# A DeltaNet and maxout kernel on one core: the output product of the last two token groups in seven half-size products instead of eight

## The chip, the cores and the metric

The kernel runs on one core of a Trainium2 chip. The metric is the time of one execution on the device in microseconds (us), the median of several executions. A profiled execution of the same program gives the durations that are used below; all of them are of one run.

## The reference

Four batches, eight heads, 768 positions and a head dimension of 48. A DeltaNet recurrence makes `y`; its heads side by side are 3072 tokens of 384 values; a maxout layer of width 768 with three weights and an output weight follows. Everything is float32.

```python
for t in range(S):
    y[:, :, t] = einsum('bhd,bhde->bhe', q[:, :, t], state)
    v_old = einsum('bhde,bhd->bhe', state, k_n[:, :, t])
    state = state + beta_t * einsum('bhd,bhe->bhde', k_n[:, :, t], v[:, :, t] - v_old)
x = y.transpose(0, 2, 1, 3).reshape(B * S, H * D)          # 3072 x 384
h = maximum(maximum(x @ w1, x @ w2), x @ w3)               # 3072 x 768
out = h @ w_out                                            # 3072 x 384
```

## The kernel before

The sequence is cut into 12 chunks of 64 positions. Two chunks of all four batches make a group of 512 tokens; there are six groups, `m` = 0 to 5. The recurrence of a group and the maxout layer of the group before it are written out in turns: `ffn(m)` (L903) is a generator that yields after each piece of the layer, and the loop at L1173 puts, after yield number `i`, the pieces of the recurrence of group `m + 1` that the table `LINKS` (L1064) names for `i`. The whole order is by hand; each engine executes its own instructions in the order in which they were written, and waits on semaphores where another engine has to be done.

In group 4, whose turns hold the recurrence of group 5, these entries matter. `s0 y0` at 8: the state update (L789) and `y` of chunk 10. `k1 q1` at 10: the products of keys and queries with the state (L731). `u1 w0` at 11: the product `p_u` (L759), and the four reads by which `y` of chunk 10 comes back from DRAM in another order (`read_y`, L850, on SP's queue). `y1 x1` at 13: the product `p_y` (L801), the addition that makes `y` of chunk 11 (L803, VectorE), and its two writes to DRAM (`y_blocks`, L839, SP's queue). `X0 w1` at 14: the transpose of chunk 10 into `xt` (`turn_y`, L861, VectorE), and the four reads of chunk 11. `X1` at 17: the transpose of chunk 11 into `xt`. Group 5 cannot start before it: its layer reads `xt` of 512 tokens at once. Group 5 itself has no recurrence beside it.

The layer of a group has two parts. In the first, each of six tiles of the hidden width has, from group 1 on, two products `p_h` of 128x128 weights with 512 tokens (L914, three matmuls each): w1 was subtracted from w2 and w3 early in the kernel, so the maximum is a relu of the first difference (L924, ScalarE) and a maximum of that with the second (L928, VectorE), and what w1 adds is put back in the output. So twelve of the yields, 0 to 11, are those of the twelve products.

The second part (L938 to L956) makes the output for the four tiles of 128 tokens: a sum of nine matmuls `p_o` with 384 columns each, six of the hidden tiles `h` with `wo_sb` (the output weight), and three of `xt` with `w_sb[0]`, whose columns 0 to 383 hold w1 times w_out since group 1 (`both_layers`, L891). Its columns 384 to 767 are not read after that. ScalarE copies each sum out (L952), and two DMAs on SP's queue store it (L955). Each of the four has a yield inside and one at its end: yields 12 to 19.

`p_h` and `p_o` take turns in two PSUM banks (`ps_ffn`, L80): a tile takes the bank of the tile two before it, once that has been read. Tiles of the pools `work` are handed on in the same way; `tmp` (L543) has two buffers in the solver of the recurrence, where one instruction writes it (L552) and the next reads it (L556). A float32 matmul of the source is two MATMUL instructions in the trace, each with its own weight load (LDWEIGHTS); a transpose is one.

Of the kernel before, what the change touches and what calls it, by code (L numbers as in the profile page):

```python
# [9 lines left out]
FP32 = mybir.dt.float32  # L10
# [4 lines left out]
ALU = mybir.AluOpType  # L15

C = 64
# [6 lines left out]
def kernel(  # L24
# [31 lines left out]
    nc = tc.nc  # L56

    B, H, S, D = q.shape
    NCH = S // C
    DM = H * D  # L60
    DFF = moe_w1.shape[1]
    KT = DM // 128
    FT = DFF // 128
    NP = H // 2
    UNITS = NCH * 2
    GROUPS = UNITS // 4
# [5 lines left out]
    work = ctx.enter_context(tc.tile_pool(name="work", bufs=2))  # L72
# [7 lines left out]
    def ps_ffn(shape, name):  # L80
        return psum.tile(shape, FP32, name=name, tag="ffn", bufs=2)
# [27 lines left out]
    def rows(bb):  # L109
        return slice(C * bb, C * (bb + 1))  # L110
# [70 lines left out]
    for bb in range(2):  # L181
        nc.gpsimd.affine_select(
            out=mask[rows(bb)], in_=mask[rows(bb)], pattern=[[1, C]], base=-1,
# [4 lines left out]
    t1 = [const.tile([128, 2, H, BL], FP32, name=f"t1{i}") for i in range(NU)]  # L188
# [5 lines left out]
    w_sb = [const.tile([128, KT, DFF], FP32, name=f"w{i}_sb") for i in range(3)]  # L194
    wo_sb = const.tile([128, FT, DM], FP32, name="wo_sb")
    pieces = []
    for f in range(FT):
        for w_t, w in zip(w_sb, (moe_w1, moe_w2, moe_w3)):
            bits = w.bitcast(U32).rearrange("(p t) f -> p t f", p=128)
            cols = slice(f * 128, (f + 1) * 128)  # L200
# [106 lines left out]
    def square(name):  # L307
        return work.tile([128, H, C], FP32, name=name, tag="square", bufs=17)
# [39 lines left out]
    def load_blocks(n, queue=nc.gpsimd):  # L348
        c, g = divmod(n, 2)
        for i in range(2):  # L350
            if n % 4 == 2:
                t = kmore[i].rearrange("p a h d -> p (a h d)")[:, 0 : 2 * TURNED]
                t = t.rearrange("p (b x) -> p b x", b=2)
            else:
                t = work.tile(
                    [128, 2, TURNED], FP32, name="turned", tag="w_bits", bufs=5
                )
            turned[n, i] = t
            nc.gpsimd.memset(t[:, :, TURNED - 48 : TURNED], 0.0)  # L359
            for bb in range(2):  # L360
                for par in range(2):
                    for db in range(2):
                        p0, at = DP * par + 32 * db, 32 * (1 - db)
                        (queue, nc.gpsimd)[i].dma_start(  # L364
                            out=t[p0 : p0 + 32, bb, at : at + NP * 2 * D].rearrange(
                                "p (j x) -> p j x", j=NP
                            ),
                            in_=(k, q)[i][
                                2 * bb + g, :, c * C : (c + 1) * C, :
                            ].rearrange(  # L370
                                "(j two) (r tb) d -> two r j (tb d)", two=2, tb=2
                            )[par],
                        )
# [69 lines left out]
    def in_rows(t):  # L443
        return t.rearrange("p s r -> p (s r)")[:, 0 : BL * BL].rearrange(
            "p (j i) -> p j i", i=BL
        )
# [51 lines left out]
    def solve(m):  # L498


        x = in_rows(xs[m])
# [38 lines left out]
        for j in range(size - 1):  # L540
            a, b = j + 1, size - 1 - j
            n = BL // size
            tmp = work.tile([128, 256], FP32, name="tmp")  # L543
            t_v = tmp[:, 0 : n * a * b].rearrange("p (s c i) -> p s c i", s=n, i=b)
            row, column, rest = (
                xv[:, :, j, None, j + 1 : size],
                yv[:, :, 0:a, j, None],
                yv[:, :, 0:a, j + 1 : size],
            )
            if n == 1:  # L550
                row, column, rest, t_v = (t[:, 0] for t in (row, column, rest, t_v))
            nc.vector.tensor_tensor(  # L552
                out=t_v, in0=row.to_broadcast(t_v.shape),
                in1=column.to_broadcast(t_v.shape), op=ALU.mult,
            )
            nc.vector.tensor_tensor(out=rest, in0=rest, in1=t_v, op=ALU.subtract)  # L556
            if m == 1 and j == BL - 8:
                nc.scalar.copy(done[:, :, 0:HB], y[:, :, 0:HB])
            elif m == 1 and j == BL - 2:
                nc.vector.tensor_copy(done[:, :, HB:BL], y[:, :, HB:BL])  # L560
            yield
        if m == 0:
# [3 lines left out]
            for i in range(4):  # L566
                if i % 2:
                    n = H * (i == 3)
# [7 lines left out]
        for cc in range(2):  # L576
            nc.sync.dma_start(
                out=y_d[cc].rearrange("f b h i j -> (f b h) i j"),
                in_=done[64 * cc : 64 * (cc + 1)],
            )  # L580
        yield
        for cc in range(2):
            for half in range(2):
                for bb in range(2):
                    r0 = C * bb + BL * half
                    (one_queue if m or cc else both_queues)[bb].dma_start(
                        out=ut[cc][
                            r0 : r0 + BL, :, :, BL * half : BL * (half + 1)
                        ].rearrange("p g h i -> p (g h) i"),
                        in_=y_d[cc, half, 2 * bb : 2 * bb + 2].rearrange(  # L590
                            "b h c i -> c (b h) i"
                        ),
# [126 lines left out]
    xts, rhss, qss, us, yts = {}, {}, {}, {}, {}  # L719
# [171 lines left out]
    def both_layers(t):  # L891
        p_m = ps_ffn([128, DM], "p_m")
        for f in range(FT):
            nc.tensor.matmul(  # L894
                p_m,
                w_sb[0][:, t, f * 128 : (f + 1) * 128],
                wo_sb[:, f],
                start=(f == 0),
                stop=(f == FT - 1),
            )  # L900
        nc.scalar.copy(w_sb[0][:, t, 0:DM], p_m)

    def ffn(m):  # L903
        xt = xts[m]
        hs = {}

        def hidden(f, lo, w):
            if f not in hs:
                hs[f] = square("h").rearrange("p h c -> p (h c)")
            h = hs[f][:, lo : lo + w]  # L910
            for i in range(m > 0, 3):
                p_h = ps_ffn([128, TOK], "p_h")[:, 0:w]
                for t in range(KT):
                    nc.tensor.matmul(  # L914
                        p_h,
                        w_sb[i][:, t, f * 128 : (f + 1) * 128],
                        xt[:, t, lo : lo + w],
                        start=(t == 0),
                        stop=(t == KT - 1),
                    )  # L920
                if i == 0:
                    nc.scalar.copy(h, p_h)
                elif m and i == 1:
                    nc.scalar.activation(  # L924
                        out=h, in_=p_h, func=mybir.ActivationFunctionType.Relu
                    )
                else:
                    nc.vector.tensor_tensor(out=h, in0=h, in1=p_h, op=ALU.max)  # L928
                yield


        early = FT // 2 if m == 0 else 0
        for lo in (0, TOK // 2):
            for f in range(early):
                yield from hidden(f, lo, TOK // 2)
        for f in range(early, FT):
            yield from hidden(f, 0, TOK)
        for i in range(4):  # L938
            cc, g = divmod(i, 2)
            p_o = ps_ffn([128, DM], "p_o")  # L940
            last = slice(i * 128, (i + 1) * 128)
            terms = [(hs[f][:, last], wo_sb[:, f]) for f in range(FT)]
            if m:
                terms += [(xt[:, t, last], w_sb[0][:, t, 0:DM]) for t in range(KT)]
            for n, (stays, moves) in enumerate(terms):
                nc.tensor.matmul(  # L946
                    p_o, stays, moves, start=(n == 0), stop=(n == len(terms) - 1)
                )
                if m and n == 4:
                    yield  # L950
            o_sb = work.tile([128, DM], FP32, name="o_sb")
            nc.scalar.copy(o_sb, p_o)  # L952
            for bb in range(2):
                tok0 = (2 * bb + g) * S + (2 * m + cc) * C
                nc.sync.dma_start(out=out[tok0 : tok0 + C, :], in_=o_sb[rows(bb)])  # L955
            yield  # L956
# [3 lines left out]
    def some(gen, n):  # L960
        for _ in range(n):
            if next(gen, gen) is gen:
                break
# [74 lines left out]
    for _ in range(2):  # L1038
# [50 lines left out]
        t=turn, K=load_k, L=lambda n: load_blocks(n, nc.sync),  # L1089
        g=lambda n: gram(n, queues=(nc.gpsimd,) * 2 if n in (10, 11) else one_queue),  # L1090
# [82 lines left out]
    for m in range(1, GROUPS):  # L1173
        for i, _ in enumerate(ffn(m)):
            if i == 0:
                some(solving, 3)
            if m == 1 and i in (2, 5, 8):
                both_layers(i // 3)
            if m + 2 < GROUPS:
                if i == 6:  # L1180
                    blocks(m + 2)
                if i == 8:
                    solving = solve(m + 2)
            links(m + 1, LINKS.get(i, ""))
            if i > 7:
                some(solving, 3 if i > 8 else 1)
# [29 lines left out]
```

## Time and profile before

| | us |
|---|---|
| median of 5 runs | 517.62 (515.58 to 521.85) |
| the profiled execution | 514.79 |
| its span, first to last instruction | 512.8 |
| TensorE (PE) busy in the span | 492.1 |
| VectorE (DVE) busy | 305.8 |
| ScalarE (ACT) busy | 163.3 |
| GpSimd (POOL) busy | 192.2 |

In the table of instruction groups, each row has the source line, engine and operation, the tiles (written <- read), the shape, the count, then busy time, mean ns of one, and the idle time of the engine before them:

```profile
L914 PE MATMUL p_h<-xt,w_sb 128*128 128x512 f32 (+1 forms) x522 | 217.7, 561 | 2.5 <-issue 1.8
L946 PE MATMUL p_o<-wo_sb,h 128*128 128x384 f32 x288 | 97.8, 489 | 0.0
L946 PE MATMUL p_o<-w_sb,xt 128*128 128x384 f32 x120 | 42.0, 486 | 0.0
L952 ACT COPY o_sb<-p_o 128x384 f32<-128x384 f32 x24 | 11.5, 478 | 132.1 <-PE p_o L946 126.0
out_dram<-o_sb SPq DMA_DIRECT2D x48, 96.0 KB, 2.2
```

The mean of one matmul is its latency with a modelled end; consecutive matmuls overlap, so that what one costs in a row of many is the busy time of the row by its count: 97.8 us by 288 is 340 ns. The last line is of the list of DMAs: the stores of the output, 48 of them of 96 KB, 2.2 us from issue to landing.

### The profile page before, as it was taken

To read this page: it belongs to the slowest core of one execution; us is meant where nothing else is said; L and a number is where in the kernel's file an instruction comes from. 1 tells how busy PE (TensorE), PEld (TensorE's weight loads), DVE (VectorE), ACT (ScalarE), POOL (GpSimd) and SP (SyncE) were. 2 spreads that over 40 slices of the span, in tenths; PEclk is the share of its full clock that TensorE was granted. 3 is DMA by queue.
4 is the path that set the end of the run, shared out by engine and by line. 5 is a ranking of instruction groups with operands and counts; after the bars stand their busy time and mean duration, and the time that the engine had idled before them with its cause. 6 is when DMAs were issued, how large, how long until landed. Compare 5 with 4: busy or idle time off the path is not lost.

```text
span 512.8 us, 18005 instructions
## 1 busy us (share of the span) xinstructions
PE 492.1 (96%) x7836; PEld 304.4 (59%) x7836; DVE 305.8 (60%) x689; ACT 163.3 (32%) x302; POOL 192.2 (37%) x317
## 2 busy tenths in 40 slices
PE   7678899999999999999999999999999999999996
PEld 6567678755565555565655665555655555654453
DVE  5888998869995521998644897727895331111100
ACT  5476855792431332100252201332001411011000
POOL 7425483773683908650757850513110000000000
PEclk9758899999999999999999999999999999999999
DMA  8927989772065916443845444834243102210011
GB/s 113 203 48 213 202 174 144 194 233 50 20 160 136 180 22 144 122 118 77 174 102 130 137 114 120 148 56 107 55 122 77 24 6 61 78 46 0 0 31 31
DMA packets 105277, 53.45 MB, mean 104 GB/s; under 512 B 89712, under 2 KB 98960, under 8 KB 105200
## 3 DMA queue, kind: packets, MB, share of 16 engines
q1 hardware_dynamic: 93616, 31.55, 30.6%
q0 software_dynamic: 9472, 20.37, 16.1%
q8 instruction: 61, 1.00, 0.9%
q10 hardware_dynamic: 2112, 0.39, 0.5%
q14 instruction: 16, 0.13, 0.1%
HBM read 39.17 MB, written 13.11 MB: 102 GB/s over the span
## 4 chain that ended last, share of the span: by engine, by line
PE 77%; DVE 11%; ACT 4%; DMA 4%; issue 2%; SPq 1%; POOL 0%; DVEq 0%; ACTq 0%; POOLq 0%
PE p_h L914 34%; PE p_o L946 23%; PE p_g L406 3%; PE p_u L759 3%; PE p_m L894 2%; DVE tmp L552 2%; PE p_y L801 2%; PE p_k L731 2%; DVE y_bl L556 2%; PE p_s L782 2%; PE p_t L329 2%; PE p_j L714 2%; DMA qall<-in_q_dram 2%; PE p_q L731 1%; PE p_z L701 1%
## 5 line engine op out<-in xcount | busy, mean ns | idle before, releaser
L914 PE MATMUL p_h<-xt,w_sb 128*128 128x512 f32 (+1 forms) x522 | 217.7, 561 | 2.5 <-issue 1.8
L914 PEld LDWEIGHTS p_h<-xt,w_sb 128*128 128x128 f32 x522 | 95.2, 191 | 87.2 <-issue 80.5
L946 PE MATMUL p_o<-wo_sb,h 128*128 128x384 f32 x288 | 97.8, 489 | 0.0
L928 DVE TENSOR_TENSOR h<-h,p_h 128x512 f32<-128x512 f32 (+1 forms) x48 | 29.6, 617 | 89.8 <-PE p_h L914 89.2
L946 PEld LDWEIGHTS p_o<-wo_sb,h 128*128 128x128 f32 x288 | 53.7, 190 | 35.7 <-issue 0.5
L552 DVE TENSOR_TENSOR tmp<-x_bl,y_bl 128x31 f32<-128x31 f32 (+20 forms) x139 | 51.3, 369 | 4.1
L952 ACT COPY o_sb<-p_o 128x384 f32<-128x384 f32 x24 | 11.5, 478 | 132.1 <-PE p_o L946 126.0
L556 DVE TENSOR_TENSOR y_bl<-y_bl,tmp 128x31 f32<-128x31 f32 (+20 forms) x139 | 48.5, 349 | 4.8
L924 ACT ACTIVATE h<-p_h 128x512 f32<-128x512 f32 x30 | 17.9, 597 | 88.3 <-PE p_h L914 86.7
L946 PE MATMUL p_o<-w_sb,xt 128*128 128x384 f32 x120 | 42.0, 486 | 0.0
L364 POOL DMA_DIRECT2D turned<-in_q_dram x72 | 39.1, 551 | 4.4 <-POOL turned L359 2.9
L254 POOL TENSOR_TENSOR w_sb<-mant,up 128x384 int32<-128x384 int32 x18 | 18.8, 1046 | 38.0 <-DVE mant L250 35.5
L946 PEld LDWEIGHTS p_o<-w_sb,xt 128*128 128x128 f32 x120 | 22.8, 190 | 15.9
L406 PEld LDWEIGHTS p_g<-kqt 48*64 48x64 f32 x1216 | 24.8, 143 | 9.2 <-issue 6.0
L406 PE MATMUL p_g<-kqt 48*64 48x64 f32 (+1 forms) x1216 | 27.9, 243 | 0.9 <-ACT kqt L335 0.8
L120 POOL DMA_DIRECT2D kpad<-in_k_dram x32 | 21.8, 690 | 13.9 <-issue 12.7
L789 DVE TENSOR_TENSOR st<-st,p_s 48x768 f32<-48x768 f32 (+1 forms) x18 | 17.1, 949 | 15.0 <-PE p_s L782 14.8
L139 POOL DMA_DIRECT2D v_t<-in_v_dram x14 | 11.5, 829 | 35.7 <-PE p_u L759 35.7
L390 DVE TENSOR_TENSOR pt<-p_g,mask 128x512 f32<-128x512 f32 x20 | 13.8, 689 | 16.3 <-PE p_g L406 16.3
L287 POOL TENSOR_TENSOR v_t<-v_t,nrm 128x768 f32<-128x768 f32 x12 | 17.9, 1492 | 9.0 <-DVE nrm L281 8.9
L359 POOL MEMSET turned<- 128x96 f32 x18 | 3.3, 191 | 47.7 <-DVE kqt L380 47.7
L759 PEld LDWEIGHTS p_u<-v_t,ut 64*64 64x64 f32 x768 | 13.5, 141 | 9.7 <-issue 8.3
(143 smaller groups left out, 615.6 us busy)
## 6 DMA issues: line engine op xcount, KB each, us to landing
out_dram<-o_sb SPq DMA_DIRECT2D x48, 96.0 KB, 2.2
w_bits<-in_moe_w_dram SPq DMA_DIRECT2D x9, 384.0 KB, 4.8
w_bits<-in_moe_w_dram POOLq DMA_DIRECT2D x9, 384.0 KB, 5.8
turned<-in_q_dram POOLq DMA_DIRECT2D x72, 48.0 KB, 2.8
kpad<-in_k_dram POOLq DMA_DIRECT2D x32, 96.0 KB, 6.5
y_x<-y SPq DMA_DIRECT2D x16, 192.0 KB
qall<-y_x SPq DMA_DIRECT2D x32, 96.0 KB, 2.6
v_t<-in_v_dram POOLq DMA_DIRECT2D x14, 192.0 KB, 5.1
```

What stands on the lines that cost most here:

```text
L120: queues[bb].dma_start(out=dst[rows(bb ^ g), :, 0:D], in_=src[2 * bb + g, :, c * C : (c + 1) * C, :].rearrange("h p d -> p h d"),)
L254: nc.gpsimd.tensor_tensor(out=dst.bitcast(I32), in0=mant_v.bitcast(I32), in1=up_v, op=ALU.add)
L287: nc.gpsimd.tensor_tensor(out=vts[c], in0=vts[c], in1=nrm[:, :, :, None].to_broadcast([128, 2, H, D]), op=ALU.mult,)
L364: (queue, nc.gpsimd)[i].dma_start(out=t[p0 : p0 + 32, bb, at : at + NP * 2 * D].rearrange("p (j x) -> p j x", j=NP), in_=(k, q)[i][2 * bb ...
L406: nc.tensor.matmul(p_g[rows(bb ^ (g * i)), par, c0 : c0 + C * (1 + whole)], kq[:, 0], kq if whole else kq[:, i],)
L552: nc.vector.tensor_tensor(out=t_v, in0=row.to_broadcast(t_v.shape), in1=column.to_broadcast(t_v.shape), op=ALU.mult,)
L556: nc.vector.tensor_tensor(out=rest, in0=rest, in1=t_v, op=ALU.subtract)
L759: nc.tensor.matmul(p_v[rows(bb ^ g), g, i], ut[c % NU][rows(bb), g, h], rhs[rows(bb), g, h],)
L914: nc.tensor.matmul(p_h, w_sb[i][:, t, f * 128 : (f + 1) * 128], xt[:, t, lo : lo + w], start=(t == 0), stop=(t == KT - 1),)
L924: nc.scalar.activation(out=h, in_=p_h, func=mybir.ActivationFunctionType.Relu)
L928: nc.vector.tensor_tensor(out=h, in0=h, in1=p_h, op=ALU.max)
L946: nc.tensor.matmul(p_o, stays, moves, start=(n == 0), stop=(n == len(terms) - 1))
```

## The change

The four output sums of the last two groups are replaced; groups 0 to 3 stay as they are. In `outputs(m, hs)`, the `h` of 512 tokens and 768 hidden values is taken as two by two blocks (256 tokens by 384), and the weight as two by two blocks (384 by 192). Seven products of blocks, with sums and differences of blocks before and after them, take the place of the eight of the ordinary way (Winograd's form of Strassen's method). The part of `xt` (four products of 256 tokens by 384 by 192) is added inside PSUM to four of the sums. Each product is six matmuls with 192 columns, for two tiles of 128 tokens and three tiles of the inner width, into one half each of a PSUM bank; 11 such products of six matmuls make 66, where there were 36 of 384 columns.

The two banks are held through the whole part as `p` and `q`. ScalarE copies four of the results out, VectorE makes the sums, and eight DMAs store the four blocks. `outputs` yields after each of the 11 products, so that its yields are numbers 12 to 22. `cross_weights` makes the four differences of the weight blocks on VectorE, in two parts after yields 8 and 9 of group 4: one of them in place in `wo_sb`, two in the free columns of `w_sb[0]`, one in the tiles `mant`, whose earlier use is over. `tmp` has one buffer instead of two in the whole kernel, which makes room for a new tile `m1`.

```diff
-            tmp = work.tile([128, 256], FP32, name="tmp")
+            tmp = work.tile([128, 256], FP32, name="tmp", bufs=1)
...
+    def cross_weights(part):
+        left, right = slice(0, HALF), slice(HALF, DM)
+        top, bottom = wo_sb[:, 0:PAIRS], wo_sb[:, PAIRS:FT]
+        spare = w_sb[0][:, :, DM : 2 * DM]
+        minus = nc.vector.tensor_tensor
+        if part == 0:
+            minus(out=spare[:, :, right], in0=bottom[:, :, right], in1=top[:, :, right], op=ALU.subtract)
+            minus(out=top[:, :, right], in0=top[:, :, right], in1=top[:, :, left], op=ALU.subtract)
+            return
+        minus(out=spare[:, :, left], in0=bottom[:, :, right], in1=top[:, :, right], op=ALU.subtract)
...
+        for j in range(PAIRS):
+            minus(out=fourth[j], in0=wo_sb[:, PAIRS + j, left], in1=spare[:, j, left], op=ALU.subtract)
...
+    def outputs(m, hs):
...
+        p, q = (ps_ffn([128, 2, HALF], "p_o") for _ in range(2))
+        def times(to, a, b, start=True, stop=True):
+            for g in range(2):
+                for j in range(PAIRS):
+                    nc.tensor.matmul(to[:, g], a[j][:, 128 * g : 128 * (g + 1)], b[j], ...)
...
+        times(p, a11, w["b11"])                        # yield 12
+        m1 = held("m1", 1); nc.scalar.copy(m1, p)
+        yield
...
+        for j in range(PAIRS): op(s32[j], a11[j], a21[j], minus)
+        for j in range(PAIRS): op(s14[j], a21[j], a22[j], plus)
+        times(q, a12, w["b21"], True, False)           # yield 13
+        yield
+        x_times(q, 0, 0)                               # yield 14
+        c11 = held("o_sb", 2); op(c11, m1, q, plus); store(c11, 0, 0)
+        yield
+        times(p, s32, w["t3"])                         # yield 15
+        m7 = held("o_sb", 2); nc.scalar.copy(m7, p)
+        yield
+        times(q, s14, w["t1"])                         # yield 16
+        m5 = held("up", 2); nc.scalar.copy(m5, q)
+        for j in range(PAIRS): op(s32[j], s14[j], a11[j], minus)
+        yield
+        times(p, s32, w["t2"])                         # yield 17
+        m6 = held("up", 2); nc.scalar.copy(m6, p)
+        for j in range(PAIRS): op(s14[j], a12[j], s32[j], minus)
+        yield
+        x_times(q, 0, 1, True, False)                  # yield 18
+        op(m6, m6, m1, plus); op(m7, m7, m6, plus)
+        yield
+        times(p, a22, w["t4"], True, False)            # yield 19
+        op(m6, m6, m5, plus); op(m5, m5, m7, plus)
+        yield
+        x_times(p, 256, 0)                             # yield 20
+        op(m7, m7, p, plus); store(m7, 1, 0)
+        yield
+        times(q, s14, w["b22"], False)                 # yield 21
+        op(m6, m6, q, plus); store(m6, 0, 1)
+        yield
+        x_times(p, 256, 1, True)                       # yield 22
+        op(m5, m5, p, plus); store(m5, 1, 1)
+        yield
...
+        if m >= GROUPS - 2:
+            yield from outputs(m, hs)
+            return
...
+            if m == GROUPS - 2 and i in (8, 9):
+                cross_weights(i - 8)
```

Statements that the source has on lines of their own are joined here, and the numbers of the yields are added. `op` is an elementwise VectorE instruction, `store` two DMAs on SP's queue, each of 64 partitions with two pieces of 768 bytes (before: one piece of 1536 bytes).

More of the change, by code (lines that the diff above doesn't have):

```diff
@@ L901, in both_layers @@
         nc.scalar.copy(w_sb[0][:, t, 0:DM], p_m)
+    HALF = DM // 2
+    PAIRS = FT // 2
+    crossed = {}
+    def cross_weights(part):
[4 more added lines that the diff above has]
+        if part == 0:
+            minus(
+                out=spare[:, :, right], in0=bottom[:, :, right], in1=top[:, :, right],
+                op=ALU.subtract,
+            )
+            minus(
+                out=top[:, :, right], in0=top[:, :, right], in1=top[:, :, left],
+                op=ALU.subtract,
+            )
+            return
+        minus(
+            out=spare[:, :, left], in0=bottom[:, :, right], in1=top[:, :, right],
+            op=ALU.subtract,
+        )
+        fourth = []
+        for n in range(2):
+            t = work.tile([128, DM], FP32, name="mant", bufs=2)
+            for i in range(2 - n):
+                fourth.append(t[:, HALF * i : HALF * (i + 1)])
+        for j in range(PAIRS):
+            minus(
+                out=fourth[j], in0=wo_sb[:, PAIRS + j, left], in1=spare[:, j, left],
+                op=ALU.subtract,
+            )
+        crossed.update(
+            b11=[top[:, j, left] for j in range(PAIRS)],
+            b21=[bottom[:, j, left] for j in range(PAIRS)],
+            b22=[bottom[:, j, right] for j in range(PAIRS)],
+            t1=[top[:, j, right] for j in range(PAIRS)],
+            t2=[spare[:, j, left] for j in range(PAIRS)],
+            t3=[spare[:, j, right] for j in range(PAIRS)],
+            t4=fourth,
+        )
@@ new lines, in outputs, with x_times, held, store @@
+    def outputs(m, hs):
+        xt, w = xts[m], crossed
+        a11, a21, a12, a22 = (
+            [hs[j + d][:, lo : lo + 256] for j in range(PAIRS)]
+            for d, lo in ((0, 0), (0, 256), (PAIRS, 0), (PAIRS, 256))
+        )
+        p, q = (ps_ffn([128, 2, HALF], "p_o") for _ in range(2))
+        def times(to, a, b, start=True, stop=True):
+            for g in range(2):
+                for j in range(PAIRS):
+                    nc.tensor.matmul(
+                        to[:, g], a[j][:, 128 * g : 128 * (g + 1)], b[j],
+                        start=(start and g == j == 0),
+                        stop=(stop and g == 1 and j == PAIRS - 1),
+                    )
+        def x_times(to, lo, right, start=False, stop=True):
+            times(
+                to,
+                [xt[:, t, lo : lo + 256] for t in range(KT)],
+                [w_sb[0][:, t, HALF * right : HALF * (right + 1)] for t in range(KT)],
+                start, stop,
+            )
+        def held(name, dtype_bufs):
+            return work.tile([128, 2, HALF], FP32, name=name, bufs=dtype_bufs)
+        def store(o, cc, right):
+            cols = slice(HALF * right, HALF * (right + 1))
+            s0 = (2 * m + cc) * C
+            for n in range(2):
+                nc.sync.dma_start(
+                    out=out.rearrange("(b s) d -> b s d", s=S)[
+                        2 * n : 2 * n + 2, s0 : s0 + C, cols
+                    ].rearrange("g c x -> c g x"),
+                    in_=o[rows(n)],
+                )
+        def op(to, a, b, how):
+            nc.vector.tensor_tensor(out=to, in0=a, in1=b, op=how)
+        plus, minus = ALU.add, ALU.subtract
+        times(p, a11, w["b11"])
+        m1 = held("m1", 1)
+        nc.scalar.copy(m1, p)
+        yield
+        sums = [square("s").rearrange("p h c -> p (h c)") for _ in range(PAIRS)]
+        s14, s32 = ([s[:, lo : lo + 256] for s in sums] for lo in (0, 256))
+        for j in range(PAIRS):
+            op(s32[j], a11[j], a21[j], minus)
+        for j in range(PAIRS):
+            op(s14[j], a21[j], a22[j], plus)
+        times(q, a12, w["b21"], True, False)
+        yield
+        x_times(q, 0, 0)
+        c11 = held("o_sb", 2)
+        op(c11, m1, q, plus)
+        store(c11, 0, 0)
+        yield
+        times(p, s32, w["t3"])
+        m7 = held("o_sb", 2)
+        nc.scalar.copy(m7, p)
+        yield
+        times(q, s14, w["t1"])
+        m5 = held("up", 2)
+        nc.scalar.copy(m5, q)
+        for j in range(PAIRS):
+            op(s32[j], s14[j], a11[j], minus)
+        yield
+        times(p, s32, w["t2"])
+        m6 = held("up", 2)
+        nc.scalar.copy(m6, p)
+        for j in range(PAIRS):
+            op(s14[j], a12[j], s32[j], minus)
+        yield
+        x_times(q, 0, 1, True, False)
+        op(m6, m6, m1, plus)
+        op(m7, m7, m6, plus)
+        yield
+        times(p, a22, w["t4"], True, False)
+        op(m6, m6, m5, plus)
+        op(m5, m5, m7, plus)
+        yield
+        x_times(p, 256, 0)
+        op(m7, m7, p, plus)
+        store(m7, 1, 0)
+        yield
+        times(q, s14, w["b22"], False)
+        op(m6, m6, q, plus)
+        store(m6, 0, 1)
+        yield
+        x_times(p, 256, 1, True)
+        op(m5, m5, p, plus)
+        store(m5, 1, 1)
+        yield
```

## The prediction

> **What bounds the kernel now.** I read first the busy table and the 40 slices of the page, then the chain of waits in order of time for the last 90 us, then the timeline there by engine.
>
> ```profile
> PE   7678899999999999999999999999999999999996
> DVE  5888998869995521998644897727895331111100
> PEclk9758899999999999999999999999999999999999
> ```
>
> TensorE is busy in nine tenths or more of nearly every slice, at full granted clock; VectorE is nearly empty in the last six slices, where the change lies. The chain of waits (start us, length us, what):
>
> ```profile
> 425.85 2.77 PE p_h L914 x6
> 428.62 1.08 PE p_u L759 x64
> 429.70 6.00 PE p_o L946 x18
> 435.70 1.08 PE p_y L801 x64
> 436.78 17.61 PE p_o L946 x54
> 454.39 30.90 PE p_h L914 x72
> 485.29 23.23 PE p_o L946 x72
> 508.53 0.03 ACTq L952
> 508.56 0.04 issue
> 508.60 0.48 ACT o_sb L952
> ```
>
> It is TensorE without a gap from 425 us to the last copy. So a microsecond taken from a `p_o` there is a microsecond of the time, until some wait appears. The output part of group 4 is 6.00 + 17.61 = 23.61 us, that of group 5 23.23 us, each of 72 instructions.
>
> **The matmuls.** Before, 72 instructions of 384 columns take 23.23 / 72 = 322.6 ns each; the 72 of 512 columns take 30.90 / 72 = 429.2 ns. Six of 256 columns:
>
> ```profile
> 71.77 1.46 PE L914 MATMUL p_h<-xt,w_sb 128*128 128x256 f32 x6
> 43.77 0.92 PE L820 MATMUL p_x<-ident,y 128*128 128x128 f32 x6 [0.78 <-DVE y L805]
> 43.74 0.76 PEld L820 LDWEIGHTS p_x<-ident,y 128*128 128x128 f32 x6 [0.87 <-ACT root_bl L261]
> ```
>
> One of 256 has a latency of 379 ns, so the step is (1.46 - 0.379) / 5 = 216 ns. The slope is (322.6 - 216) / 128 = 0.833 ns a column, and 512 columns lie on that line. At 192 columns it gives 216 - 64 x 0.833 = 162.7 ns. After, a group has 66 matmuls, 132 instructions: 132 x 0.1627 = 21.47 us instead of 23.23. Columns fall by a twelfth (66 x 192 against 36 x 384), and 60 more instructions give a little of that back. **Gain: 1.76 us in each group, 3.52 us in all.**
>
> That stands if the weight loads keep up. The load of a `p_o` matmul lasts 190 ns in the trace, longer than 162.7, and every matmul has its own. The third line above shows that a load's duration is not its pace: six loads of 195 ns each in 0.76 us, a step of (0.76 - 0.195) / 5 = 113 ns, at a granted clock of 1.00, with matmuls of 128 columns between. These are transposes, one instruction each, but their loads are the longer kind. The first matmuls of the kernel (`p_w`, L977), ordinary float32 with 128 columns, run slower in every part, with loads of 333 ns and latencies of 421, and 12 of them take 2.93 us: at most (2.93 - 0.421) / 11 = 228 ns a step, again well under the load. So the price of a step lies between 162.7 and 190 ns (the full duration of a load); I take 162.7, since both rows with narrower matmuls stay well under their load's duration.
>
> **Group 4, in time.** A product of six matmuls is 12 x 0.1627 = 1.95 us. With the 0.19 us that `p_o` loses at each change from the recurrence's products (6.00 - 18 x 0.3226, and the same once more in the 17.61), products 1 and 2 end at 433.80, `p_y` at 434.88, and products 3 to 11 at 437.02, 438.98, 440.93, 442.88, 444.83, 446.78, 448.74, 450.69 and 452.64. Now the waits. VectorE's prices: 384 elements 0.55 us (L871 551 ns in SBUF; between L928's 408 and 686 ns for 256 and 512 out of PSUM), 256 elements 0.42 (L552), 0.03 between two.
>
> The six sums before product 4 begin after the last maximum, at 429.45, and take 6 x 0.45 = 2.7 us: done by 432.2, needed at 437.02. The sums for product 6 wait for product 4 (438.98), come behind the transpose of chunk 10 (1.23 us from 437.7) and end at 440.5; product 6 starts at 440.93 and wants only the first of them. ScalarE's copies of four sums (0.48 us each) have a whole product's time. These cost nothing; without that cover each would cost what it is late, some tenths.
>
> The transpose of chunk 11 is another matter:
>
> ```profile
> 437.89 1.16 SPq L839 DMA_DIRECT2D y_x<-y  x2
> 444.70 2.54 SPq L850 DMA_DIRECT2D qall<-y_x  x4
> 449.07 1.25 DVE L861 STREAM_TRANSPOSE xt<-qall 128x768 f32<-128x768 f32 x1 [10.07 <-DMA qall<-y_x]
> ```
>
> `y` goes to DRAM, the reads wait for that, and VectorE stood 10.07 us before the transpose, with nothing behind it. After the change `p_y` ends 1.90 us earlier (434.88 for 436.78), so the transpose starts at 447.17 and ends at 448.42. The store of the first block is now queued on SP between the writes and the reads; it goes out by 438.9 and the reads wait until 442.8 anyway. But behind the transpose VectorE now has four sums of 384 (2.32 us, to 450.77) and then the sum that reads bank `p` after product 9, done at 451.32. Product 11 writes that bank and should start at 450.69: with 0.05 us for the semaphore it starts at 451.37. **Stall: 0.68 us**, from none (transpose 0.7 us earlier) to some 2.2 (1.5 later, since a store of 192 KB, now in smaller pieces, shares the queue with the writes).
>
> Product 11 ends at 453.32, and the first `p_h` of group 5 takes the same bank `p`: it waits for the last sum, 0.13 us (the time from `p_y`'s end to its reader, 436.91 - 436.78) + 0.55 + 0.05 = **0.73 us**. Before, the bank of the next tile had been read a product earlier. `p_h` starts at 454.05 instead of 454.39: group 4 gains 0.35.
>
> The Trainium skill, "Perfetto Trace Analysis", section Optimizing Tensor Performance, says that independent groups of matmuls should rotate through banks so that a copy overlaps the next group. The place just priced breaks that rotation once; the rows above give its cost, the page gives none.
>
> **Group 5.** No recurrence stands between, so the same order has no late transpose; the sum out of `p` after product 9 starts at once, a product ahead of its need. At the end VectorE's sum (0.13 + 0.55) stands where ScalarE's copy stood (0.07 + 0.48): +0.13. The two last stores are of the same size and the issue took 0.56 us for 128 rows (L839) and 0.59 for 64 (L955), so I take the tail of DMA as unchanged (0 to 0.5 more). Group 5 gains 1.76 - 0.13 = 1.63.
>
> **At nothing.** The weight differences: in part one, two instructions of 576 elements, 0.75 us each (from 551 ns for 384 and 1225 for 1024, L538), in VectorE's wait of 2.71 us before the state update at 417.63; part two, 0.75 + 3 x 0.35 + gaps = 1.9 us, after the maximum that ends at 422.06 and before the subtraction at 425.04, an idle of 2.98. If that cover were gone, up to 1.5 us would fall on `p_u`. The single `tmp`: each multiplication in the solver waits for the subtraction before it already, since it reads the row that it wrote; both stand in one engine's order. SP's other stores have nobody behind them.
>
> **Sum.** -0.35 - 1.63 = -1.98 us: 512.8 for the profiled execution of 514.79 us. The median of the runs is 0.55% above that execution, so the same ratio gives 515.6 against 517.62.
>
> **Rivals.** (1) *The loads set the pace: slower.* At 190 ns a step a group's products take 25.08 us, 1.85 more than before; the stall at product 11 disappears (its bank is read in time), the wait of the first `p_h` and the tail stay: 2 x 1.85 + 0.73 + 0.13 = +4.56, 522.2 us. It decides from about 170 ns a step (1.98 us over 264 instructions above 162.7). For it: the load lasts longer than the matmul, in ordinary matmuls at full clock never seen before. Against: the two rows of narrow matmuls. Chance 0.10.
> The harder form of it, load and matmul one after the other, would be 190 + 162.7 ns a step, 46.6 us a group and some 564 us; chance 0.01, as 72 instructions with loads of 190 ns already go by at 322.6, on the line of the columns alone. The Trainium skill, "TensorE: Matmul & The Clock Gate", section Part 3, has that form as a rule: a load overlaps running matmuls only where their row groups differ. By that rule the present step could not be what it is, all loads being of 128 rows; the trace disagrees.
> (2) *The late transpose costs more.* If `y` returns 1.5 us later than I shift it, product 11 and group 5 start that much later: 514.3 and, scaled, 517.1. For it: the write waits 5.6 us on its landing and now shares the time with a store. Chance 0.22.
> (3) *No stall at product 11*, the transpose 0.7 us or more earlier: 0.68 less, 514.9. Chance 0.13.
> That the change does not do what it says is excluded: the built order has 66 matmuls of 192 columns in each of the two groups.
>
> **How the numbers follow.** My forecast has 0.50; 0.04 is for what I have not seen, on both sides. About 1% is what a measurement of this kernel can tell from no change: the runs before lie between -0.4% and +0.8% of their median. All likely cases lie within 1%. Slower by over 1%: half of rival 1, which stands at +0.9%, its harder form, and a little of rival 2 and the unseen: 0.08. Faster by over 1%: the forecast at -0.4% and rival 3 at -0.5% with the scatter of a median, and the unseen: 0.07. Range: from 3 us below the forecast (no stall, and 2 us of scatter) to 519.6, which takes in rival 2 with its scatter and leaves out most of rival 1.
>
> **What would show it.** The `p_o` of group 5 in the chain of waits at about 21.5 us with 132 instructions, its loads starting about 163 ns apart; VectorE's transpose of chunk 11 near 447 and idle on the DMA; product 11 of group 4 waiting on VectorE for some 0.7 us, and the first `p_h` of group 5 for as much. Wrong if group 5's part is 25 us, if the `p_h` before the output part grow, or if the stores at the end land later than 2.2 us after issue.

## The result, and the profile after

| | us |
|---|---|
| median before / after | 516.81 / 515.92 |
| ratio of the runs after to those before | 0.9981, 95% interval 0.9969 to 0.9992 |
| forecast | 515.6 (512.6 to 519.6) |
| the profiled execution after, and its span | 517.23, 515.3 |

The change makes the kernel about 1.0 us faster (0.19% of 516.81; 0.4 to 1.6 by the interval). The profiled execution after happens to be longer than that of before; it is 3.4 us late already at 433.12 us, where the output part of group 4 begins (429.70 before), and 2.7 us of that are there at 98.5 us (the first instruction of L871, 95.8 before), long before the output parts that were changed. The other profiles read here begin the part between 430.4 and 434.4 us (three_groups aside), the kernel with nothing but the single `tmp` buffer latest, so the stretches are compared from there on. The profile of the run named after_again fell into a disturbed execution (granted clock 0.83) and is not read below; its times are.

The chain of waits in order of time of the changed kernel (start us, length us, what):

```profile
432.04 1.08 PE p_u L759 x64
433.12 2.16 PE p_o L960 x12
435.28 0.02 issue
435.30 0.49 ACT m L994
435.79 2.63 issue
438.42 0.96 DVE y L803
...
439.99 6.43 DMA y_x<-y
...
447.76 1.70 SPq L850
...
449.51 2.58 DMA qall<-y_x
...
452.11 1.22 DVE xt L861
...
455.66 0.57 DVE o_sb L989
...
456.27 2.22 PE p_o L960 x12
458.49 30.90 PE p_h L1057 x72
489.38 21.46 PE p_o L960 x132
510.85 0.02 issue
510.87 0.56 DVE up L989
```

Before, this stretch was TensorE alone. Now the chain leaves TensorE in the first products of group 4 and goes through `y` of chunk 11, its way to DRAM and back, the transpose and VectorE's sums, and returns to TensorE only for product 11. (The 2.63 us called issue are a gap in what the chain could follow: meanwhile TensorE ran product 2 and `p_y`, which ended at 437.14 + 1.15 = 438.29 us, just before VectorE made `y`.) Group 4 took 454.39 - 429.70 = 24.69 us from the end of `p_u` to the first `p_h` of group 5; it takes 458.49 - 433.12 = 25.37: 0.68 us more. Group 5's 132 instructions take 21.46 instead of 23.23 us, 1.77 less. From the last matmul to the end of the span it is 515.3 - 510.85 = 4.45 us, before 512.8 - 508.53 = 4.27: 0.18 more. Together 0.68 - 1.77 + 0.18 = -0.91 us, or 0.9982 of the 514.79 of the profiled execution before, inside the measured interval.

The timeline by engine (start us, length us, engine, line, work, count, in brackets the idle before and what ended it):

```profile
437.14 1.15 PE L801 MATMUL p_y<-u,pt 64*64 64x48 f32 x64
446.48 3.64 SPq L850 DMA_DIRECT2D qall<-y_x  x4
452.11 1.22 DVE L861 STREAM_TRANSPOSE xt<-qall 128x768 f32<-128x768 f32 x1 [7.29 <-DMA qall<-y_x]
453.26 0.52 DVE L989 TENSOR_TENSOR up<-up,m 128x384 f32<-128x384 f32 x1
453.81 0.56 DVE L989 TENSOR_TENSOR o_sb<-o_sb,up 128x384 f32<-128x384 f32 x1
454.40 0.56 DVE L989 TENSOR_TENSOR up<-up 128x384 f32<-128x384 f32 x1
454.99 0.56 DVE L989 TENSOR_TENSOR up<-up,o_sb 128x384 f32<-128x384 f32 x1
455.66 0.56 DVE L989 TENSOR_TENSOR o_sb<-o_sb,p_o 128x384 f32<-128x384 f32 x1
458.52 0.56 DVE L989 TENSOR_TENSOR up<-up,p_o 128x384 f32<-128x384 f32 x1 [1.85 <-PE p_o L960]
456.27 2.22 PE L960 MATMUL p_o<-w_sb,xt 128*128 128x192 f32 x12 [2.18 <-DVE o_sb L989]
458.32 1.88 PE L1057 MATMUL p_h<-xt,w_sb 128*128 128x512 f32 x4
```

VectorE stands 7.29 us before the transpose, and four sums and the one that frees bank `p` come behind it. Product 11 waits 2.18 us for that sum. The last two lines hold a second thing: the first `p_h` of group 5 writes from 458.32 on, before the sum of 458.52 has read bank `p`. So it uses the other bank, `q`, and does not wait for that sum.

### The profile page after: what moved, and what is told of

Read it like the earlier page. It is cut to its first block, busy times and chain, and to the rows that moved or that the text cites. A ratio compares the mean times of both kernels' runs of the same rounds, so it can differ in the third digit from the quotient of the medians.

```text
span 515.3 us, 18314 instructions
## 1 busy us (share of the span) xinstructions
PE 493.7 (96%) x7956; PEld 322.6 (63%) x7956; DVE 325.7 (63%) x735; ACT 163.5 (32%) x302; POOL 192.7 (37%) x317
## 4 chain that ended last, share of the span: by engine, by line
PE 81%; DVE 7%; DMA 5%; ACT 2%; issue 2%; SPq 1%; POOL 0%; DVEq 0%; POOLq 0%; ACTq 0%
PE p_h L1057 37%; PE p_o L1092 17%; PE p_o L960 5%; PE p_g L406 4%; DMA qall<-in_q_dram 3%; PE p_u L759 2%; PE p_m L894 2%; PE p_k L731 2%; PE p_s L782 2%; PE p_j L714 2%; PE p_y L801 2%; PE p_q L731 1%; PE p_t L329 1%; PE p_z L701 1%; DMA y_x<-y 1%
## 5 line engine op out<-in xcount | busy, mean ns | idle before, releaser
L1092 PE MATMUL p_o<-wo_sb,h 128*128 128x384 f32 x192 | 65.3, 490 | 0.0
L1092 PEld LDWEIGHTS p_o<-wo_sb,h 128*128 128x128 f32 x192 | 35.7, 190 | 23.2
L1098 ACT COPY o_sb<-p_o 128x384 f32<-128x384 f32 x16 | 7.7, 478 | 86.1 <-PE p_o L1092 80.0
L1092 PE MATMUL p_o<-w_sb,xt 128*128 128x384 f32 x72 | 25.2, 486 | 0.0
L1092 PEld LDWEIGHTS p_o<-w_sb,xt 128*128 128x128 f32 x72 | 13.7, 190 | 9.5
L960 PE MATMUL p_o<-w_sb,xt 128*128 128x192 f32 x96 | 17.1, 328 | 2.2 <-DVE o_sb L989 2.2
```

Source lines behind the costliest of these rows:

```text
L960: nc.tensor.matmul(to[:, g], a[j][:, 128 * g : 128 * (g + 1)], b[j], start=(start and g == j == 0), stop=(stop and g == 1 and j == PAIRS - 1),
L1092: nc.tensor.matmul(p_o, stays, moves, start=(n == 0), stop=(n == len(terms) - 1))
```

## The experiments

Each is the changed kernel with the edit shown, unless it says otherwise; the edits are shown shortened. A ratio is against the kernel before on the same chip. "Group 4's part" is the time from the end of `p_u` to the first `p_h` of group 5.

**The parts alone.** First the changed kernel again, then the seven products in one of the two groups.

> The changed kernel once more, beside the parts of it. Theory A (the matmuls gain 1.76 us in each group; in group 4 the wait for the late transpose of chunk 11 takes more than that back): group 5's output part again 21.46 us, group 4's between the end of p_u and the first p_h of group 5 about 25.4 us (24.7 before), and some 1.0 us less in the ratio (0.998). Theory B (the stall of 2.2 us before product 11 was an accident of that one profile, in which one read of y took 1.70 us to issue instead of 0.60): group 4's part about 24 us here.

Ratio 0.9938 (0.9910 to 0.9966): below the 0.998 of theory A; theory B gives both groups 0.996 (under g5_only).

```diff
-        if m >= GROUPS - 2:
+        if m == GROUPS - 2:
             yield from outputs(m, hs)
...
+            if m == GROUPS - 1 and i == 8:      # wo_sb as it was
+                nc.vector.tensor_tensor(out=top_right, in0=top_right, in1=top_left, op=ALU.add)
```

> The seven products in group 4 alone; group 5 is made in the old way, after one more instruction on VectorE restores the block of wo_sb that was changed in place. Theory A: group 4's part is 0.7 us longer than before, nothing else moves, so +0.7 us (ratio 1.001). Theory B: group 4's part gains about 0.4 to 1.1 us (ratio 0.998 to 0.999).

Ratio 1.0001 (0.9975 to 1.0027). Chain and timeline of this kernel:

```profile
430.53 1.08 PE p_u L759 x64
456.82 30.90 PE p_h L1057 x72
487.72 23.23 PE p_o L1092 x72
454.61 2.22 PE L960 MATMUL p_o<-w_sb,xt 128*128 128x192 f32 x12 [2.02 <-DVE o_sb L989]
444.95 3.54 SPq L850 DMA_DIRECT2D qall<-y_x  x4
```

Group 4's part is 456.82 - 431.61 = 25.21 us, 0.52 more than before, with a wait of 2.02: the stall is no accident of one profile. The seven products in group 4, in this order, gain nothing.

```diff
-        if m >= GROUPS - 2:
+        if m >= GROUPS - 1:
             yield from outputs(m, hs)
...
-            if m == GROUPS - 2 and i in (8, 9):
+            if m == GROUPS - 1 and i in (8, 9):
                 cross_weights(i - 8)
```

> The seven products in group 5 alone (the weight differences are made on VectorE in group 5). Theory A: the whole gain lies here: 1.76 us less for the matmuls, 0.2 us more at the end, -1.6 us (ratio 0.997), more than both groups together. Theory B: less than both groups together, ratio 0.997 against 0.996 for both.

Ratio 0.9972 (0.9945 to 1.0000), group 5 again 21.46 us, group 4 as before (458.22 - 433.52 = 24.70). So the trace is as theory A has it. The times do not bear it out: by A this kernel gains more than both groups together, and on this chip both together came out lower (0.9938), with intervals that overlap.

**The late transpose out of the way.** One entry of the order is moved: the transpose of chunk 11 (`X1`) from behind yield 17 to behind yield 20, where the sum that frees bank `p` already stands in VectorE's order:

```diff
-            links(m + 1, LINKS.get(i, ""))
+            names = LINKS.get(i, "")
+            if m == GROUPS - 2:
+                names = {17: "", 20: "X1"}.get(i, names)
+            links(m + 1, names)
```

> The changed kernel with one thing moved: in group 4 the transpose of chunk 11 stands on VectorE behind the sum that frees bank p after product 9 (yield 20 instead of 17). Theory A: product 11 no longer waits, 2.2 us less than the changed kernel, group 4's part about 23.2 us, -3.1 us against before (ratio 0.994). Theory B: nothing or up to 0.7 us less than the changed kernel. A third theory (the first p_h of group 5 waits for xt instead, since the transpose now ends later): the stall moves to the first p_h and the time stays at 0.998.

Ratio 0.9945 (0.9920 to 0.9970), as theory A gave it. Its timeline and chain:

```profile
450.24 0.56 DVE L989 TENSOR_TENSOR o_sb<-o_sb,p_o 128x384 f32<-128x384 f32 x1 [2.95 <-PE p_o L960]
450.71 1.22 DVE L861 STREAM_TRANSPOSE xt<-qall 128x768 f32<-128x768 f32 x1
431.17 4.10 PE p_o L960 x24
435.27 1.08 PE p_y L801 x64
436.35 17.75 PE p_o L960 x108
454.10 30.90 PE p_h L1057 x72
485.00 21.46 PE p_o L960 x132
```

TensorE is the chain again without a gap; group 4's part is 454.10 - 431.17 = 22.93 us, 1.76 less than before, just the gain that was worked out for the matmuls, and 25.37 - 22.93 = 2.44 us less than in the changed kernel: the wait of 2.18 us, and 0.27 us that product 11 took longer behind it. The transpose finds its data already there, and `p_h` does not wait for it. Since the changed kernel had come out alike in the same comparison (0.9938), both were measured once more on one chip.

> The changed kernel once more, on one chip with x1_late, as the two came out alike in the first comparison (0.994 both) although the traces show a stall of 2.2 us in one and none in the other. Theory A (the stall is real and costs its length): ratio about 0.998 here. Theory B (it is there in some executions only, or is paid back elsewhere): the same ratio as x1_late. The trace: 1.4 to 2.2 us of wait before product 11 of group 4.

Ratio 0.9978 (0.9952 to 1.0005); the wait before product 11 is 1.99 us.

> Theory A: about 2 us less than the changed kernel on the same chip, ratio 0.994. Theory B: as the changed kernel. The trace: no wait before product 11, group 4's part 22.9 us, group 5's 21.46.

Ratio 0.9928 (0.9894 to 0.9962), no wait, group 4's part 455.65 - 432.73 = 22.92 us. So theory A: in the traces the stall costs its length and a little more. The times bear this out in this comparison (0.9978 and 0.9928, with intervals that still overlap a little) and did not in the first (0.9938 and 0.9945). The 0.9938 of the changed kernel stands beside 0.9981, the most exact, and 0.9978; what made it so low is not known, and a comparison of this size is uncertain by some 0.3% either way.

**What made the transpose late.** The store of the first block is moved behind the reads on SP's queue, with the transpose in its old place:

```diff
         op(c11, m1, q, plus)
-        store(c11, 0, 0)
         yield
+        store(c11, 0, 0)
         times(p, s32, w["t3"])
```

> The changed kernel with the store of the first block queued on SP behind the four reads of chunk 11 instead of before them. The theory (the store shares the way with the write of y and delays its landing, and with it the transpose and product 11): from the write's issue to the first read 6.8 us as before the change (7.05 with the store between), so the transpose starts 0.25 us earlier relative to p_y; if the third read issues in 0.6 us too (1.7 in the profile of the changed kernel), 1.3 us earlier and the stall at product 11 falls to about 0.9 us. The rival (the write's time does not depend on the store): 7.05 us and a stall of 1.0 or 2.1 us, depending on the third read alone.

One execution (514.88 us; the kernel before beside it 516.52, the median of 7):

```profile
438.00 1.14 SPq L839 DMA_DIRECT2D y_x<-y  x2
444.81 2.53 SPq L850 DMA_DIRECT2D qall<-y_x  x4
449.89 1.24 DVE L861 STREAM_TRANSPOSE xt<-qall 128x768 f32<-128x768 f32 x1 [6.46 <-DMA qall<-y_x]
454.05 2.22 PE L960 MATMUL p_o<-w_sb,xt 128*128 128x192 f32 x12 [1.36 <-DVE o_sb L989]
```

From the write's issue to the first read it is 444.81 - 438.00 = 6.81 us, as before the change (444.70 - 437.89), against 446.48 - 439.40 = 7.08 with the store between. The theory holds for that quarter of a microsecond, and the other profiles read here bear it out: this time is 7.00 to 7.10 us in the eight with the store between, 6.79 to 6.81 in the five without. The four reads issue in 2.53 us here and 3.64 in the changed kernel, and the wait falls to 1.36, not to the 0.9 expected: the reads land later, 449.89 - 447.34 = 2.55 us after the last issue instead of 452.11 - 450.12 = 1.99. The store now shares the time with the reads; that this is the reason was not tried. Both moves at once:

> Both moves at once. With the transpose out of the way of the sums nobody waits for the reads any more, so the store's place should not matter: as x1_late within the interval, ratio 0.994. If it is faster than x1_late by over 1 us, something in the store's place costs that these traces do not show.

Ratio 0.9948 (0.9915 to 0.9980): as x1_late within the interval; once nobody waits for the reads, no effect of the store's place shows.

**The bank.** As x1_late, with VectorE's last two sums in the other order, so that bank `q` is freed after `p`:

```diff
-        op(m6, m6, q, plus)
-        store(m6, 0, 1)
         yield
         x_times(p, 256, 1, True)
         op(m5, m5, p, plus)
         store(m5, 1, 1)
+        op(m6, m6, q, plus)
+        store(m6, 0, 1)
```

> As x1_late, but the sum that frees bank q (after product 10) stands on VectorE behind the sum that frees bank p (after product 11), and both before group 5. The prediction gave the first p_h of group 5 a wait of 0.73 us, as the next tile would take bank p; in the traces it did not wait. Theory: the next tile takes the bank that was freed first, q, and the wait appears once no bank is freed before product 11 ends: the first p_h of group 5 starts some 0.7 us after product 11's last matmul. Rival: the bank was p all along and was free early for another reason: no wait here either.

The timeline:

```profile
452.24 2.11 PE L960 MATMUL p_o<-w_sb,xt 128*128 128x192 f32 x12
454.39 1.02 DVE L989 TENSOR_TENSOR up<-up,p_o 128x384 f32<-128x384 f32 x2 [2.21 <-PE p_o L960]
455.00 2.41 PE L1057 MATMUL p_h<-xt,w_sb 128*128 128x512 f32 x5 [0.65 <-DVE up L989]
```

The wait is there, 0.65 us, once no bank is free before product 11 ends, and it ends with the first of the two sums, the one that reads `p`. So the tile takes the bank that is freed first: `q` in the changed kernel, `p` here, and not always that of the tile two before it, as the description of the kernel has it.

**Where the loads begin to bound.** As x1_late, each matmul of group 5's output part cut in two:

```diff
-                    nc.tensor.matmul(to[:, g], a[j][...], b[j], ...)
+                    for c in range(0, HALF, cols):      # cols = 96 in group 5
+                        nc.tensor.matmul(to[:, g, c : c + cols], a[j][...], b[j][:, c : c + cols], ...)
```

> As x1_late, with each matmul of group 5's output part cut into two of 96 columns: the same columns, twice the weight loads, 264 instructions. If the columns alone set the pace (0.833 ns each and about 2.5): 83 ns a step, 21.8 us. If a load takes the pace that six transposes showed (113 ns, or 109 in others): 28.8 to 29.8 us, +7.4 to +8.4 us against x1_late. If a load blocks for its whole 190 ns: 50 us.

```profile
456.15 30.90 PE p_h L1060 x72
487.05 29.47 PE p_o L962 x264
```

29.47 / 264 = 111.6 ns a step, where the columns alone would give 83, so something else sets the pace. It is no fixed cost of every instruction: the 64 small products of `p_y`, each with a load of its own, take 1.08 us, 17 ns each. The loads of 128x128, which last 190 to 192 ns here and come every 112, are the likeliest, but no run separates them from another cost of matmuls of this size. The 113 ns of the six transposes do not decide it: on the line of the columns (216 - 128 x 0.833) their 128 columns alone give 109.

**One group more.** The seven products in groups 3 to 5, the second transpose late in groups 3 and 4 (`m >= GROUPS - 3`, and the weight differences two groups before the last).

> The seven products in groups 3, 4 and 5, the transpose of the second chunk late in groups 3 and 4. In group 3 VectorE is busy 22.2 of 25 us, with the solver for group 5 in its order. Theory: the 7.5 us of sums and differences that the change adds there find 2.8 us of idle, VectorE becomes the bound of that group and gives back more than the 1.8 us that the matmuls gain: 2 to 6 us slower than x1_late, ratio about 0.998 to 1.006. Rival (VectorE's order has slack that the busy time does not show, as nobody waits for the solver there): 1.8 us faster than x1_late, ratio 0.991.

Ratio 1.0138 (1.0066 to 1.0211): slower, by more than expected. The profile is of the longest of its five executions (529.53 us; the median is 525.18). The timeline of TensorE in group 3, and the window table (us, busy us of PE, PEld, DVE, ACT and POOL with instructions, granted clock, DMA share, GB/s):

```profile
376.83 2.11 PE L960 MATMUL p_o<-w_sb,s 128*128 128x192 f32 x12
383.67 4.21 PE L960 MATMUL p_o<-wo_sb,s 128*128 128x192 f32 x12 [4.73 <-DVE o_sb L989]
390.46 4.18 PE L960 MATMUL p_o<-w_sb,s 128*128 128x192 f32 x12 [2.59 <-DVE s L989]
394.43 2.76 PE L960 MATMUL p_o<-w_sb,xt 128*128 128x192 f32 x12
...
372.00:400.00 28.00, 20.69 (x214) 19.63 (x213) 26.58 (x65) 1.44 (x3) 4.20 (x5) 0.76 0.20 51
```

VectorE, at 26.58 of 28 us, has the sums between the steps of the solver; products wait 4.73 and 2.59 us for them, and the products after these waits take twice their time. The granted clock is 0.76 in the mean of the stretch: 1.00 until 379.0 us, 0.83 over the first wait (379.0 to 383.6), 0.50 from there through the second wait to 395.5, and 1.00 again from 397.0. From the first `p_o` of group 3 to the first `p_h` of group 4 it is 404.83 - 368.88 = 35.95 us; before it was 386.15 - 360.83 = 25.32.

**The single `tmp`**, on the kernel before:

```diff
-            tmp = work.tile([128, 256], FP32, name="tmp")
+            tmp = work.tile([128, 256], FP32, name="tmp", bufs=1)
```

> The kernel before with the single tmp buffer and nothing else. The prediction gave it nothing: each multiplication in the solver waits for the subtraction before it in any case. Ratio 1.000; if the two buffers hid something, up to some tenths of a us at each of 139 steps on VectorE, which would show as over 1.01.

Ratio 1.0017 (0.9988 to 1.0046): nothing that can be told from no change. That alone would leave up to 2.4 us open, but the rows of the solver's two instructions are the same in the profile of the kernel before and in this one, to the last digit, in busy time and in idle time before them:

```profile
L552 DVE TENSOR_TENSOR tmp<-x_bl,y_bl 128x31 f32<-128x31 f32 (+20 forms) x139 | 51.3, 369 | 4.1
L556 DVE TENSOR_TENSOR y_bl<-y_bl,tmp 128x31 f32<-128x31 f32 (+20 forms) x139 | 48.5, 349 | 4.8
```

## Why the prediction was right, and where its steps failed

The matmuls: 132 instructions of 192 columns take 21.46 us (21.47 worked out), and 1.76 us less in group 4 as well where nothing stalls (x1_late). Loads of 190 ns do not slow a pace of 162.6; half_columns shows a floor, at 112 ns and not at 190. Rival 1 and its harder form are excluded.

Group 5 and the tail: 1.77 - 0.18 = 1.59 gained, 1.63 expected.

Group 4 was forecast to gain 0.35 us and loses 0.68. Two steps were wrong, in opposite directions. "**Stall: 0.68 us**": the place, the mechanism and the waiting instructions were right (x1_late removes it), its size was not: 2.18 us. The transpose was shifted with `p_y` as if the way of `y` took as long as before. From the start of `p_y` (435.63 us before) to the transpose it was 449.07 - 435.63 = 13.44 us and is 452.11 - 437.14 = 14.97. Of these 1.53 us, 0.27 lie in the write's landing beside the store (shown by store_late), 1.10 in the issue of the four reads (3.64 for 2.54 us; nearly all in the third, which takes 1.70), and 0.16 in their landing. So by the trace it is rival 2 that came about, at its price of 1.5 us; it had a chance of 0.22, and its reason, the store, accounts for a small part.

Why one read issues slowly stays open. The four reads took 3.50 to 3.65 us in five profiles with the seven products in group 4 and 2.53 to 2.55 in five others. In each of the slow five, a fetch of instructions by DMA starts within 0.1 us of the start of the slow read, the third in two of them and the fourth in three. In the fast five there is none during the reads (three_groups), or it starts 0.35 to 0.47 us into the last one. But such a fetch is not enough: in after_third, a read at 359.30 us takes 0.60 us with a fetch at its start. Nor does it take the seven products: a read of 1.80 us stands in tmp_alone, in another group. No run moves the fetch.

"The first `p_h` of group 5 takes the same bank `p`": wrong. The trace shows it writing before `p` was read, and q_last that the tile takes the bank that is freed first; the wait that the prediction priced at 0.73 us was not there, and is 0.65 where it is forced. Besides, product 11 takes 2.22 us after its wait instead of 1.95. So -0.35 becomes -0.35 + 1.50 - 0.73 + 0.27 = +0.69, as measured.

The errors cancel only in part: -1.98 us forecast, -0.91 by the trace, -0.4 to -1.6 by the interval. The gain is about half of the forecast one, and the forecast ratio (515.6 / 517.62 = 0.9961) lies outside the measured interval. That 515.92 came out so near 515.6 is in part luck: the forecast set out from 517.62, the median of five executions, and the larger measurement has 516.81. All of the gain comes from group 5. The edits costed at nothing show no cost: the weight differences end before the next step of the recurrence needs VectorE (x1_late has no gap in the chain from there on), and `tmp` makes no difference in the solver's rows.

The best version by the traces is x1_late, 2.8 and 3.7 us (ratios 0.9945 and 0.9928) below the kernel before: the same change, with one transpose three yields later. That it is also faster than the changed kernel shows in the times of one comparison of two.

## What to carry to other kernels

A saving in matmuls is paid in VectorE instructions; before spending them, look at what else stands in that engine's order. An instruction that waits for a transfer holds all that is queued behind it, and work put behind it inherits its wait: place it behind whatever somebody waits for sooner. Where VectorE is full, as in group 3 here, the same change costs several times what it saves (10.6 us lost where 1.8 were to be saved).

## What the runs showed that was not expected

A float32 load of 128x128 that lasts 190 ns is repeated every 112 ns when the matmuls are short: its duration is no pace. Matmuls of 192 columns (162.6 ns a step) are clear of that floor, those of 96 are not.

After a wait of TensorE of 4.73 us in three_groups the granted clock was 0.50 and the products went at half the pace (4.2 us for 2.1) for some 12 us, the second wait of 2.59 us included. After the single wait of 2.18 us in the changed kernel it stayed at 1.00, and product 11 took 2.22 us. So a wait can cost more than its length; how long it must be for that, two cases do not say.
